# Two attention blocks on one core: PSUM tiles of the first chunks, and when the filler bank may open

## The chip, the cores and the metric

The kernel runs on one core of a Trainium2 chip. The metric is the device time of one execution in microseconds (us). The kernel before was run seven times: median 1201.62 us, lowest 1192.62, highest 1206.26 (all: 1192.62, 1201.62, 1206.26, 1194.90, 1203.48, 1195.62, 1204.34). One further execution was recorded by the hardware profiler.

Engines are named as in the profile: PE (TensorE matmul), PEld (its weight load), DVE (VectorE), ACT (ScalarE), POOL (GpSimd), SP (SyncE, which issues most transfers).

## What is computed

Two multi-head attention blocks, A and B, on different inputs of the same shape (2048 tokens, 512 features, 32 heads of 16). A attends to all tokens; B to the last 256 up to the token itself. The outputs stand side by side.

```python
qkv = (x @ wqkv).reshape(B, S, 3, H, Dh)          # S 2048, D 512, H 32, Dh 16
scores = einsum("bhqd,bhkd->bhqk", q, k) * Dh ** -0.5
# B only: scores = where(0 <= row - col < 256, scores, -1e9)
p = softmax(scores, axis=-1)
o = einsum("bhqk,bhkd->bhqd", p, v)
out = o.transpose(0, 2, 1, 3).reshape(B, S, D) @ wo
return concatenate([A, B], axis=-1)
```

## The kernel before, in words

**Jobs and slots.** A job is one head, one tile of 128 keys and up to 512 queries. Heads go in eight groups of four (`g`), queries in four passes of 512 (`p`), so a unit (instance, pass, group) of A has 64 jobs. Three jobs make a slot; there are 811 slots, and the first 21 belong to group 0 of pass 0 of A. `run` (L690) goes through them in order. In iteration s it issues: the exponentials of slot s on ACT (`exps`, L466, from PSUM tile `sps`, three banks, two buffers, into SBUF tile `pT`), the scores of slot s+2 on PE (`scores`, L448), the products with the values of earlier slots (`values`, L500, into the one-bank PSUM tile `op`), due pieces of the epilogue (`later`), then filler, and last a guard if one is due. Instructions keep this order on each engine.

**The warm matmul.** The scores of a job use 32 rows of the array; three of them stand side by side. Ahead of each slot's scores L443 issues one matmul over all 128 rows whose result is overwritten.

**Filler.** Everything else that PE must do goes into one PSUM bank, `ms` (`bank`, L113, one buffer): projections of K, Q and values, and the output projection. `pair` (L245) cuts each of these into two steps of two matmuls: the first opens the bank, the second finishes the sum and has it copied out. `plan` (L615) gives each task a due slot; `fill` (L677) issues one step of the first task that may run. `run` computes per slot the rate that the due slots ask for, adds it to `credit` (at most 2.0), and issues one step for each whole credit. A Q projection is followed two slots later by a `guard` (L304 or L400): a further matmul into `ms` whose result becomes an extra row that bounds the exponent. It is issued behind the filler of its slot, if no bank stands open.

**Padded K and Q.** The scores want each head's 16 rows at a distance of 32. Later groups get this by a trip through DRAM: the projection is copied out (L217, L297), written to scratch (`kd`, `qd`), and read back three slots later. The first two groups (`gg` 0 and 1) of A, with all keys and the first 512 queries, get it at once from padded weights `wpad` (`pad_mm`, L372). `pad_k_evac` (L382) moves the K bank to `kT` on ACT (L384, adding the constant `ones16`) and takes its largest magnitude on DVE (L386). `pad_guard` (L400) reduces and scales on DVE, then a matmul L408 and an addition L410 into the Q tile. Group 0 is done in `start`; group 1 is the task `pad` of `plan` (four K chunks, one Q), due six slots ahead of slot 21.

**The start (L550).** The tokens of A come in four chunks of 512 (L559), alternately on SP's and ACT's queue. For each chunk a three-bank `sps` tile is taken: eight transposes (L577) into its first bank, a copy by ACT to `xT`, eight into the second, a copy by DVE (L581), then four matmuls of padded K (L199) into the third, and L384 and L386. With chunk 0 the padded Q is done in `ms`. Then come the guard of group 0 and six value tiles (L594), three to an `sps` tile, each copied by ACT (L281). Then `run` issues the scores of slots 0 and 1.

**Priorities around the change.** K of pair `pr` is due 28 slots ahead of its first use, Q 22 slots ahead, value tile t of A one slot ahead, the pad task 6 slots ahead of slot 21.

Of the kernel before, what the change touches and what calls it, by code (L numbers as in the profile page):

```python
# [90 lines left out]
class _Kernel:  # L91

    def __init__(self, ctx, tc, tensors, out):
        self.tc, self.nc = tc, tc.nc
        self.t = tensors
        self.out = out
        pool = lambda name, **kw: ctx.enter_context(tc.tile_pool(name=name, **kw))
        self.consts = pool("consts", bufs=1)
        self.sb = pool("sb", bufs=1)
        self.ps = pool("ps", bufs=1, space=bass.MemoryType.PSUM)  # L100
        self.dram = pool("dram", bufs=1, space=bass.MemoryType.DRAM)
        self.xT, self.w, self.wo, self.kT, self.v, self.qT = {}, {}, {}, {}, {}, {}
        self.acol, self.negas, self.oT = {}, {}, {}
        self.op, self.od = {}, {}
        self.later = []
        self.slot = self.ended = -1
        self.pend, self.guards = [], []
        self.open = None

    def tile(self, shape, dt, tag, bufs):  # L110
        return self.sb.tile(shape, dt, name=tag, tag=tag, bufs=bufs)
# [5 lines left out]
    def constants(self):  # L117

        nc = self.nc
        pick = nc.gpsimd.affine_select  # L120
        warm = self.consts.tile([1, 1], FP32, name="warm")
        nc.vector.memset(warm[:], 0.0)
        nc.scalar.activation(out=warm[:], in_=warm[:], func=ACT.Exp)
        self.ident = self.consts.tile([P, P], BF16, name="ident")
        nc.gpsimd.memset(self.ident[:], 1.0)
        pick(self.ident[:], self.ident[:], pattern=[[1, P]], compare_op=ALU.is_equal,
             fill=0.0, base=0, channel_multiplier=-1)
        self.wpad = self.consts.tile([P, 2, NC, 2, P], BF16, name="wpad")
        nc.gpsimd.memset(self.wpad[:].bitcast(FP32), 0.0)

        sel = self.consts.tile([P, GH], FP32, name="sel")
        nc.gpsimd.memset(sel[:], 1.0)
        pick(sel[:], sel[:], pattern=[[-32, GH]], compare_op=ALU.is_equal, fill=0.0, base=-DH,
             channel_multiplier=1)
        self.ones16 = self.consts.tile([P, 1], FP32, name="ones16")
        nc.vector.reduce_sum(out=self.ones16[:], in_=sel[:], axis=AX.X)
        self.padsel = self.consts.tile([P, P], BF16, name="padsel")
        p3 = self.padsel[:].rearrange("p (j r) -> p j r", r=32)
        nc.gpsimd.memset(self.padsel[:], -1.0)
        pick(p3, p3, pattern=[[0, GH], [1, 32]], compare_op=ALU.is_equal, fill=0.0, base=-DH,  # L140
             channel_multiplier=0)
        pick(p3, p3, pattern=[[-32, GH], [0, 32]], compare_op=ALU.is_ge, fill=0.0, base=0,
             channel_multiplier=1)
        pick(p3, p3, pattern=[[32, GH], [0, 32]], compare_op=ALU.is_ge, fill=0.0, base=DH - 1,
             channel_multiplier=-1)
# [99 lines left out]
    def pair(self, first, second):  # L245

        def f():
            self.open = self.bank()
            first(self.open[:])

        def g():
            bank, self.open = self.open, None
            second(bank[:])
        return [f, g]

# [125 lines left out]

    def pad_k_evac(self, gg, c, bank):  # L382
        kT, o = self.kT[0, 0, c]
        self.nc.scalar.activation(out=kT[:, gg, o:o + 512], in_=bank, func=ACT.Identity,  # L384
                                  scale=1.0, bias=self.ones16[:])
        self.nc.vector.tensor_reduce(out=self.padmax[:, gg, c:c + 1], in_=bank, axis=AX.X,  # L386
                                     op=ALU.max, apply_absolute_value=True)

# [28 lines left out]
    def pad_steps(self):  # L417

        steps = []
        for c in range(NPASS):  # L420
            def second(bank, c=c):
                self.pad_mm(1, 1, c, bank, (2, 3))
                self.pad_k_evac(1, c, bank)
            steps += self.pair(lambda bank, c=c: self.pad_mm(1, 1, c, bank, (0, 1)), second)

        def q_second(bank):
            self.pad_mm(0, 1, 0, bank, (2, 3))
            mq = self.pad_q_evac(1, bank)
            self.guards.append((self.slot + 2, lambda: self.pad_guard(1, mq)))
        steps += self.pair(lambda bank: self.pad_mm(0, 1, 0, bank, (0, 1)), q_second)  # L430
        return steps


    def scores(self, slot):
        sps = self.ps.tile([P, SLOT, 512], FP32, name="sps", tag="sps", bufs=2)
        for b, jb in enumerate(slot["jobs"]):
            r = slice(32 * jb.j, 32 * jb.j + KR)
            qT = self.qT[jb.inst, jb.p, jb.g // 2]
            gg = jb.g % 2
            if b == 0:  # L440

                kT, k0 = self.kT[jb.inst, jb.g // 2, jb.subs[0][0] // 4]
                self.nc.tensor.matmul(sps[:, 0, 0:WARM], lhsT=kT[:, gg, k0:k0 + P],  # L443
                                      rhs=qT[:, gg, 0:WARM], start=True, stop=True)
            for kt, q0, q1, o in jb.subs:
                kT, k0 = self.kT[jb.inst, jb.g // 2, kt // 4]
                k0 += (kt % 4) * P
                self.nc.tensor.matmul(sps[:, b, o:o + q1 - q0],  # L448
                                      lhsT=kT[r, gg, k0:k0 + P],
                                      rhs=qT[r, gg, q0:q1], start=True, stop=True,  # L450
                                      tile_position=(32 * jb.j, 0))
        slot["sps"] = sps
# [97 lines left out]
    def start(self):  # L550
# [5 lines left out]
        self.load_w(0, 1, nc.scalar, (0, P))  # L556
        self.load_w(0, 0, nc.sync, (0, P))
        for c in range(NPASS):
            (nc.sync if c % 2 == 0 else nc.scalar).dma_start(xs[c // 2][:, c % 2], x[:, c])  # L559
        self.load_w(0, 2, nc.sync)  # L560
        self.load_w(0, 1, nc.scalar, (P, D))
        self.load_w(0, 0, nc.sync, (P, D))
# [3 lines left out]
                self.pad_w(n, gg)  # L566
        self.padmax = self.consts.tile([P, 2, NPASS], FP32, name="padmax")
        self.k_begin(0, 0, 0)
        for c in range(NPASS):
            big = self.ps.tile([P, SLOT, 512], FP32, name="sps", tag="sps", bufs=2)  # L570
            xT = self.tile([P, NC, 512], BF16, "xT", XRING)
            self.xT[0, c] = xT
            for h in range(2):
                tb = big[:, h, :].bitcast(BF16).rearrange("p (d n) -> p d n", d=2)
                for d in range(2):
                    for k in range(4):
                        nc.tensor.transpose(tb[:, d, k * P:(k + 1) * P],  # L577
                                            xs[c // 2][:, c % 2, k, (2 * h + d) * P:
                                                       (2 * h + d + 1) * P], self.ident[:])
                copy = nc.vector.tensor_copy if h else nc.scalar.copy  # L580
                copy(out=xT[:, 2 * h:2 * h + 2, :], in_=tb)  # L581
            self.pad_mm(1, 0, c, big[:, 2, :], range(NC))
            self.pad_k_evac(0, c, big[:, 2, :])
            if c == 0:
                b = self.bank()
                self.pad_mm(0, 0, 0, b[:], range(NC))
                mq = self.pad_q_evac(0, b[:])
        self.pad_guard(0, mq)
        self.qT[0, 0, 0] = self.padq
        nv = 2 * SLOT  # L590
        for t0 in range(0, nv, SLOT):
            vb = self.ps.tile([P, SLOT, 512], FP32, name="sps", tag="sps", bufs=2)
            for t in range(t0, t0 + SLOT):
                self.v_mm(0, t, vb[:, t - t0, :], range(NC))  # L594
                self.v_evac(0, t, vb[:, t - t0, :], nc.scalar.copy)
        self.more_constants()
        self.load_wo(0)
        return [("v", 0, t) for t in range(nv)] + [("k", 0, 0), ("q", 0, 0, 0)]
# [16 lines left out]
    def plan(self, slots, done):  # L615
# [23 lines left out]
        for t in range(NKT):  # L639
            task(("v", 0, t), vneed[0, t] - 1, self.v_steps(0, t))  # L640
        for pr in range(NPAIR):
            task(("k", 0, pr), begin[0, 0, 2 * pr] - 28, self.k_steps(0, pr, range(NPASS)))
        for i in range(2):
            for p, pr in q_order:
                old = before(q_order, (p, pr), QRING[i])
                task(("q", i, p, pr), begin[i, p, 2 * pr] - 22, self.q_steps(i, p, pr),
                     [("k", 0, pr)] if i == 0 else [("k", 1, p, pr), ("w", 1, 0)],
                     old and (i, old[0], 2 * old[1] + 1))
            for p in range(NPASS):
# [27 lines left out]
    def fill(self, s, tasks, done):  # L677

        if self.open is None:
            self.cur = next((t for t in tasks if t["nb"] <= s and t["after"] <= done), None)  # L680
            if self.cur is None:
                return False
# [7 lines left out]
    def run(self):  # L690
# [6 lines left out]
        for s, sl in enumerate(slots):  # L697
# [11 lines left out]
            for t in tasks:  # L709
                if t["nb"] <= s:  # L710
                    total += len(t["steps"])
                    rate = max(rate, total / max(1, t["due"] - s))
            credit = min(credit + min(rate, 2.0), 2.0)
            while credit >= 1.0 and self.fill(s, tasks, done):
                credit -= 1.0
            if self.guards and self.guards[0][0] <= s and self.open is None:
                self.guards.pop(0)[1]()
        finish = self.last_out(0, NPASS - 1)
        while self.pend:
            self.slot += 1  # L720
# [54 lines left out]
```

## Time and profile before

| what | us |
|---|---|
| median of seven runs | 1201.62 |
| profiled execution, its own time | 1196.32 |
| its span | 1194.6 |
| ACT busy | 1102.5 |
| PE busy (ends are modelled) | 944.6 |
| DVE busy | 293.3 |
| POOL busy | 120.0 |
| first exponential starts | 44.31 |
| exponential of slot 22 starts | 98.86 |
| mean granted PE clock, share of full | 0.941 |

How to read what follows. The slices of the page cut the span into 40 equal parts of 29.9 us, each digit the busy share in tenths. A row of the groups gives line, engine, operation, result and inputs, count, then busy us and mean ns, then the engine's idle time just ahead of these instructions and what ended most of it. A row of the waits reads: who waited, for whom, us in total, times, the longest. A row of the timeline reads: start in us, duration, engine, line, operation; in brackets how long the engine had been idle and what released it. Busy time by stretch:

| stretch, us | PE | DVE | ACT | POOL |
|---|---|---|---|---|
| 0 to 10 | 2.03 | 3.17 | 2.50 | 8.53 |
| 10 to 20 | 7.19 | 3.42 | 1.70 | 5.70 |
| 20 to 30 | 6.10 | 2.77 | 3.40 | 0 |
| 30 to 40 | 6.59 | 1.79 | 2.45 | 0 |
| 40 to 50 | 7.56 | 1.37 | 7.33 | 0 |
| 50 to 60 | 9.76 | 4.16 | 8.03 | 0 |
| 60 to 70 | 7.64 | 4.82 | 4.03 | 0 |
| 70 to 80 | 5.77 | 1.38 | 4.06 | 0 |
| 80 to 90 | 7.88 | 2.27 | 6.21 | 0 |
| 90 to 100 | 8.62 | 4.46 | 6.94 | 0 |
| 100 to 120 | 16.36 | 4.13 | 20.00 | 0 |

### The profile page before, as it was taken

To read this page: it belongs to the slowest core of one execution; us is meant where nothing else is said; L and a number is where in the kernel's file an instruction comes from. 1 tells how busy PE (TensorE), PEld (TensorE's weight loads), DVE (VectorE), ACT (ScalarE), POOL (GpSimd) and SP (SyncE) were. 2 spreads that over 40 slices of the span, in tenths; PEclk is the share of its full clock that TensorE was granted. 3 is DMA by queue.
4 is the path that set the end of the run, shared out by engine and by line. 5 is a ranking of instruction groups with operands and counts; after the bars stand their busy time and mean duration, and the time that the engine had idled before them with its cause. 6 is when DMAs were issued, how large, how long until landed. Compare 5 with 4: busy or idle time off the path is not lost.

```text
span 1194.6 us, 17547 instructions
## 1 busy us (share of the span) xinstructions
PE 944.6 (79%) x6944; PEld 272.4 (23%) x6944; DVE 293.3 (25%) x665; ACT 1102.5 (92%) x849; POOL 120.0 (10%) x316
## 2 busy tenths in 40 slices
PE   5778787887788888878788888788887888787893
PEld 3212222222222222222222222222222222222221
DVE  3223111113222213312232232133222332310101
ACT  2548999999999999999999999999999999999993
POOL 4000000001001000211011120012110111200100
PEclk9879999989999998999999999998999999979777
DMA  5011323022231202211240212123102221110101
GB/s 193 18 54 41 101 69 94 10 72 64 71 82 46 78 18 83 64 53 39 69 118 19 66 62 63 51 77 92 49 15 74 82 67 55 56 50 32 56 19 54
DMA packets 72746, 73.87 MB, mean 62 GB/s; under 512 B 22624, under 2 KB 55768, under 8 KB 72664
## 3 DMA queue, kind: packets, MB, share of 16 engines
q1 hardware_dynamic: 69624, 68.83, 19.1%
q10 hardware_dynamic: 2400, 1.84, 0.5%
q0 software_dynamic: 640, 2.10, 0.4%
q8 instruction: 54, 0.88, 0.3%
q14 instruction: 28, 0.23, 0.1%
HBM read 39.06 MB, written 31.58 MB: 59 GB/s over the span
## 4 chain that ended last, share of the span: by engine, by line
ACT 62%; PE 23%; issue 11%; DVE 2%; DMA 1%; ACTq 0%; SPq 0%; DVEq 0%
ACT pT L466 61%; PE sps L448 6%; PE sps L443 6%; PE ms L199 5%; PE op L500 4%; PE sps L199 1%; DVE osb L519 1%; PE sps L577 1%; DMA kTa<-in_A_x_dram 0%; ACT xT L581 0%; DVE pT L477 0%; PE sps L354 0%; DMA rb<-rd 0%; ACT kTa L384 0%; ACT va L281 0%
## 5 line engine op out<-in xcount | busy, mean ns | idle before, releaser
L466 ACT ACTIVATE pT<-sps 128x1536 bf16<-128x1536 f32 (+4 forms) x827 | 1087.2, 1559 | 26.0 <-PE sps L448 25.1
L443 PE MATMUL sps<-qTa,kTa 128*128 128x512 bf16 x683 | 268.3, 393 | 174.2 <-ACT pT L466 169.0
L448 PE MATMUL sps<-qTa,kTa 32*128 32x512 bf16 x2048 | 284.0, 400 | 0.0
L500 PE MATMUL op<-pT,va 128*32 128x512 bf16 x2048 | 214.2, 407 | 0.3 <-DVE osb L519 0.2
L479 POOL TENSOR_SCALAR_AFFINE_SELECT pT<-pT 128x256 bf16<-128x256 bf16 (+2 forms) x224 | 103.6, 481 | 990.2 <-issue 558.4
L448 PEld LDWEIGHTS <-kTa 32*128 32x128 bf16 x2048 | 68.1, 91 | 407.7 <-issue 407.7
L477 DVE TENSOR_TENSOR pT<-pT,mlo 128x256 bf16<-128x256 bf16 (+2 forms) x256 | 74.4, 332 | 144.0 <-ACT pT L466 142.7
L443 PEld LDWEIGHTS <-kTa 128*128 128x128 bf16 x683 | 66.6, 97 | 145.9 <-issue 124.3
L500 PEld LDWEIGHTS <-va 128*32 128x32 bf16 x2048 | 53.4, 94 | 123.3 <-issue 123.0
L443 PE MATMUL sps<-qTb,kTb 128*128 128x512 bf16 x128 | 51.7, 404 | 33.6 <-ACT pT L466 32.0
L519 DVE COPY osb<-op 128x512 f32<-128x512 f32 x64 | 44.2, 691 | 91.3 <-PE op L500 91.2
L448 PE MATMUL sps<-qTb,kTb 32*128 32x384 bf16 (+2 forms) x704 | 59.0, 292 | 0.0
L217 DVE CAST kst<-ms 128x512 bf16<-128x512 f32 x28 | 19.4, 692 | 133.9 <-PE ms L199 133.9
L339 DVE CAST ob<-ms 128x512 bf16<-128x512 f32 x28 | 19.3, 691 | 133.7 <-PE ms L199 133.7
L297 DVE CAST qs<-ms 128x512 bf16<-128x512 f32 x31 | 21.4, 690 | 105.7 <-PE ms L199 105.7
L199 PE MATMUL ms<-xT,wq 128*128 128x512 bf16 x124 | 41.5, 421 | 0.3 <-DVE gs L308 0.3
L500 PE MATMUL op<-pT,vb 128*32 128x384 bf16 (+2 forms) x704 | 36.4, 289 | 1.9 <-DVE osb L519 1.6
L448 PEld LDWEIGHTS <-kTb 32*128 32x128 bf16 x704 | 17.0, 93 | 79.1 <-issue 79.1
L199 PE MATMUL ms<-xT,wk 128*128 128x512 bf16 x112 | 34.0, 392 | 0.2 <-DVE kst L217 0.2
L281 DVE CAST vb<-ms 128x512 bf16<-128x512 f32 x16 | 11.1, 692 | 85.2 <-PE ms L199 85.2
L199 PE MATMUL ms<-wv,xT 128*128 128x512 bf16 x104 | 30.1, 387 | 0.7 <-DVE va L281 0.5
L308 DVE CAST gs<-ms 8x512 bf16<-8x512 f32 x31 | 20.9, 676 | 19.5 <-PE ms L306 19.5
(76 smaller groups left out, 290.8 us busy)
## 6 DMA issues: line engine op xcount, KB each, us to landing
od<-osb SPq DMA_DIRECT2D x64, 256.0 KB
oc<-od SPq DMA_DIRECT2D x32, 256.0 KB
rb<-rd SPq DMA_DIRECT2D x32, 256.0 KB
kTb<-kd SPq DMA_DIRECT2D x16, 256.0 KB
qTb<-qd SPq DMA_DIRECT2D x16, 256.0 KB
qd<-qs SPq DMA_DIRECT2D x31, 128.0 KB
qTa<-qd SPq DMA_DIRECT2D x15, 256.0 KB
out_dram<-ob SPq DMA_DIRECT2D x30, 128.0 KB
```

The costliest lines, as they stand in the source:

```text
L199: self.nc.tensor.matmul(bank, lhsT=lhs(c), rhs=rhs(c), start=(c == 0), stop=(c == NC - 1))
L217: copy(out=kst[:], in_=bank)
L297: copy(out=qs[:], in_=bank)
L308: self.nc.vector.tensor_copy(out=gs[:], in_=b[0:8, :])
L339: self.nc.vector.tensor_copy(out=ob[:], in_=bank)
L443: self.nc.tensor.matmul(sps[:, 0, 0:WARM], lhsT=kT[:, gg, k0:k0 + P], rhs=qT[:, gg, 0:WARM], start=True, stop=True)
L448: self.nc.tensor.matmul(sps[:, b, o:o + q1 - q0], lhsT=kT[r, gg, k0:k0 + P], rhs=qT[r, gg, q0:q1], start=True, stop=True, tile_position=(3 ...
L466: nc.scalar.activation(out=pT[:, b:e, :n], in_=sps[:, b:e, :n], func=ACT.Exp, scale=SCALE)
L477: nc.vector.tensor_mul(out=v, in0=v, in1=self.mlo[:, 0:e - b, :])
L479: nc.gpsimd.affine_select(v, v, pattern=[[0, e - b], [-1, P]], compare_op=ALU.is_ge, fill=0.0, base=-1, channel_multiplier=1)
L500: self.nc.tensor.matmul(op[32 * jb.j:32 * jb.j + 32, q0:q1], lhsT=self.v[jb.inst, kt][:, h * VP:h * VP + 32], rhs=slot["pT"][:, b, o:o + q ...
L519: nc.vector.tensor_copy(out=osb[:], in_=self.op[i, p, g][:])
```

## The change

- **Token loads.** Each chunk is loaded in two halves, one on SP's queue and one on ACT's.
- **Busy array.** 24 matmuls of 256 columns on constants (`hum`, zeros, new) into `ms` stand ahead of the first transposes on PE. Their result is not used.
- **The chunks.** All sixteen transposes of a chunk are issued together (`turn`), the two copies after them (`keep`). K chunks go to `op` and `ms` in turn (`keys`), no longer to the third bank of `sps`. The order on PE is: transposes of chunk c, then K of chunk c-1; the padded Q follows K of chunk 0.
- **Values.** Two value tiles instead of six are made in the start, each in `op`; the guard of group 0 stands between them. The other four join the filler.
- **Padded K of group 1** is moved to `kT` by DVE instead of ACT; the group 0 stays on ACT.
- **Warm matmul.** L443 is left out in slots whose preceding iteration issued two or more filler steps, and in slots 0 and 1.
- **The bank.** After a step that closes `ms`, or a guard, no new pair opens in that slot. The guard is issued ahead of the filler of its slot. The credit may rise by 2.5 a slot and to 3.0.
- **Due slots.** K is due 16 slots ahead instead of 28; Q of pass 0 of A 14 instead of 22.

```diff
@@ pair
         def g():
             bank, self.open = self.open, None
+            self.closed = self.slot
             second(bank[:])
@@ pad_k_evac
-        self.nc.scalar.activation(out=kT[:, gg, o:o + 512], in_=bank, func=ACT.Identity,
-                                  scale=1.0, bias=self.ones16[:])
+        if gg == 0:
+            self.nc.scalar.activation(out=kT[:, gg, o:o + 512], in_=bank, func=ACT.Identity,
+                                      scale=1.0, bias=self.ones16[:])
+        else:
+            self.nc.vector.tensor_scalar(out=kT[:, gg, o:o + 512], in0=bank,
+                                         scalar1=self.ones16[:], scalar2=None, op0=ALU.add)
@@ scores
-            if b == 0:
+            if b == 0 and self.filled < 2:
@@ start
-            (nc.sync if c % 2 == 0 else nc.scalar).dma_start(xs[c // 2][:, c % 2], x[:, c])
+            for h, eng in enumerate((nc.sync, nc.scalar)):
+                eng.dma_start(xs[c // 2][:, c % 2, 2 * h:2 * h + 2], x[:, c, 2 * h:2 * h + 2])
...
+        def busy(n):
+
+            b = self.bank()
+            for _ in range(n):
+                nc.tensor.matmul(b[:, 0:256], lhsT=self.padsel[:], rhs=self.hum[:],
+                                 start=True, stop=True)
+
+        def turn(c):
+            big[c] = self.ps.tile([P, SLOT, 512], FP32, name="sps", tag="sps", bufs=2)
             for h in range(2):
...
+        def keep(c):
+            xT = self.tile([P, NC, 512], BF16, "xT", XRING)
+            self.xT[0, c] = xT
+            for h in range(2):
+                tb = big[c][:, h, :].bitcast(BF16).rearrange("p (d n) -> p d n", d=2)
                 copy = nc.vector.tensor_copy if h else nc.scalar.copy
                 copy(out=xT[:, 2 * h:2 * h + 2, :], in_=tb)
...
+        def keys(c):
+            b = tile_("op", 1) if c % 2 == 0 else self.bank()
+            self.pad_mm(1, 0, c, b[:], range(NC))
+            self.pad_k_evac(0, c, b[:])
+        busy(24)
+        turn(0)
+        keep(0)
+        turn(1)
+        keys(0)
+        keep(1)
+        b = self.bank()
+        self.pad_mm(0, 0, 0, b[:], range(NC))
+        mq = self.pad_q_evac(0, b[:])
+        for c in range(2, NPASS):
+            turn(c)
+            keys(c - 1)
+            keep(c)
+        keys(NPASS - 1)
+        nv = 2
+        for t in range(nv):
+            vb = tile_("op", 1)
+            self.v_mm(0, t, vb[:], range(NC))
+            self.v_evac(0, t, vb[:], nc.scalar.copy)
+            if t == 0:
+                self.pad_guard(0, mq)
+                self.qT[0, 0, 0] = self.padq
@@ plan
-            task(("k", 0, pr), begin[0, 0, 2 * pr] - 28, self.k_steps(0, pr, range(NPASS)))
+            task(("k", 0, pr), begin[0, 0, 2 * pr] - 16, self.k_steps(0, pr, range(NPASS)))
...
-                task(("q", i, p, pr), begin[i, p, 2 * pr] - 22, self.q_steps(i, p, pr),
+                task(("q", i, p, pr), begin[i, p, 2 * pr] - (14 if i + p == 0 else 22), self.q_steps(i, p, pr),
@@ fill
         if self.open is None:
+            if self.closed == s:
+                return False
@@ run
-            credit = min(credit + min(rate, 2.0), 2.0)
+            credit = min(credit + min(rate, 2.5), 3.0)
+            self.filled = 0
+            if self.guards and self.guards[0][0] <= s and self.open is None:
+                self.guards.pop(0)[1]()
+                self.closed = s
             while credit >= 1.0 and self.fill(s, tasks, done):
                 credit -= 1.0
-            if self.guards and self.guards[0][0] <= s and self.open is None:
-                self.guards.pop(0)[1]()
+                self.filled += 1
```

More of the change, by code (lines that the diff above doesn't have):

```diff
@@ L105, in __init__ @@
         self.later = []
-        self.slot = self.ended = -1
+        self.slot = self.ended = self.closed = -1
         self.pend, self.guards = [], []
         self.open = None
+        self.filled = 2
     def tile(self, shape, dt, tag, bufs):
@@ L127, in constants @@
              fill=0.0, base=0, channel_multiplier=-1)
+        self.hum = self.consts.tile([P, 256], BF16, name="hum")
+        nc.vector.memset(self.hum[:], 0.0)
         self.wpad = self.consts.tile([P, 2, NC, 2, P], BF16, name="wpad")
@@ L428, in q_second, with guard @@
             mq = self.pad_q_evac(1, bank)
-            self.guards.append((self.slot + 2, lambda: self.pad_guard(1, mq)))
+            self.padq_done = False
+            def guard():
+                self.pad_guard(1, mq)
+                self.padq_done = True
+            self.guards.append((self.slot + 2, guard))
         steps += self.pair(lambda bank: self.pad_mm(0, 1, 0, bank, (0, 1)), q_second)
@@ L439, in scores @@
             gg = jb.g % 2
-            if b == 0:
+            assert jb.key != (0, 0, 1) or self.padq_done
+            if b == 0 and self.filled < 2:
                 kT, k0 = self.kT[jb.inst, jb.g // 2, jb.subs[0][0] // 4]
@@ L568, in start @@
         self.k_begin(0, 0, 0)
[L569 to L572, printed above, removed]
+        tile_ = lambda tag, bufs: self.ps.tile([P, 512], FP32, name=tag, tag=tag, bufs=bufs)
+        big = {}
+        def busy(n):
[5 more added lines that the diff above has]
+            big[c] = self.ps.tile([P, SLOT, 512], FP32, name="sps", tag="sps", bufs=2)
             for h in range(2):
-                tb = big[:, h, :].bitcast(BF16).rearrange("p (d n) -> p d n", d=2)
+                tb = big[c][:, h, :].bitcast(BF16).rearrange("p (d n) -> p d n", d=2)
                 for d in range(2):
@@ L579, in start @@
                                                        (2 * h + d + 1) * P], self.ident[:])
+        def keep(c):
+            xT = self.tile([P, NC, 512], BF16, "xT", XRING)
+            self.xT[0, c] = xT
+            for h in range(2):
+                tb = big[c][:, h, :].bitcast(BF16).rearrange("p (d n) -> p d n", d=2)
                 copy = nc.vector.tensor_copy if h else nc.scalar.copy
                 copy(out=xT[:, 2 * h:2 * h + 2, :], in_=tb)
[L582 to L595, printed above, removed]
+        def keys(c):
[24 more added lines that the diff above has]
+                self.qT[0, 0, 0] = self.padq
         self.more_constants()
```

## The prediction, written before the changed kernel was run

> **What bounds the kernel now.** I read the page's slices first, then ScalarE's (ACT's) waits, then the timeline of the first 100 us. The page says which engine and where:
>
> ```profile
> ACT  2548999999999999999999999999999999999993
> PEclk9879999989999998999999999998999999979777
> ...
> L466 ACT ACTIVATE pT<-sps 128x1536 bf16<-128x1536 f32 (+4 forms) x827 | 1087.2, 1559 | 26.0 <-PE sps L448 25.1
> ```
>
> From the fourth slice on ACT is busy 90% or more: the 811 slots are exponentials back to back (24 of them from 98.86 us take 32.34 us, so 1.345 us a slot). 1087.2 us of exponentials is a floor that the change does not touch. Time can be won only where ACT waits: ahead of the first exponential (44.31 us), in slices 2 to 3, in scattered gaps, and in the tail. ACT's own waits:
>
> ```profile
> ACT pT L466 <- PE sps L448: 25.1, 49, 1.9
> ACT ob L364 <- PE sps L354: 16.0, 1, 16.0
> ACT kTa L384 <- PE sps L199: 14.0, 4, 3.8
> ACT kTa L384 <- PE ms L199: 12.8, 4, 3.6
> ACT va L281 <- PE sps L199: 9.9, 6, 2.6
> ```
>
> L384 into `kTa` appears twice: in the start (sps) and inside the slots (ms). The second is 12.8 us in four waits, the largest loss inside the loop. The 16.0 us is the tail, untouched. The timeline of the start shows a ring of waits:
>
> ```profile
> 9.00 1.01 PE L577 MATMUL sps<-ident,kTa 128*128 128x128 bf16 x8 [1.10 <-ACT xT L581]
> ...
> 20.16 0.69 ACT L384 ACTIVATE kTa<-sps,ones 128x512 bf16<-128x512 f32 x1 [3.81 <-PE sps L199]
> 20.88 0.69 DVE L386 TENSOR_REDUCE padmax<-sps 128x1 f32<-128x512 f32 x1 [2.67 <-ACT kTa L384]
> ```
>
> The second eight transposes wait for ACT's copy of the first eight although they write another bank of the tile; L386 waits for L384, both reading one bank. A chunk takes 5.68 us (transposes at 14.23, 19.91, 25.59). The array runs at half rate: K matmuls follow each other at 0.427 us, against 0.216 later. Now the slots:
>
> ```profile
> 53.77 1.04 PE L199 MATMUL ms<-wv,xT 128*128 128x512 bf16 x4
> ...
> 55.59 1.02 PE L199 MATMUL ms<-wv,xT 128*128 128x512 bf16 x4 [0.24 <-DVE va L281]
> ...
> 64.74 1.04 PE L199 MATMUL ms<-xT,wpad 128*128 128x512 bf16 x4
> ...
> 65.82 0.69 ACT L384 ACTIVATE kTa<-ms,ones 128x512 bf16<-128x512 f32 x1 [3.43 <-PE ms L199]
> 66.40 1.44 ACT L466 ACTIVATE pT<-sps 128x1536 bf16<-128x1536 f32 x1
> 67.90 0.59 PE L443 MATMUL sps<-qTa,kTa 128*128 128x512 bf16 x1 [2.12 <-ACT pT L466]
> ```
>
> A slot with four filler matmuls takes 1.82 us on PE: 1.04 for the matmuls to end, 0.69 for VectorE to empty the one `ms` bank, some 0.09 between. In the padded K slots ACT stands in line for the `ms` matmuls, its next exponential behind them, and PE's next scores behind that: 5 us a slot. Slot 22 starts its exponential at 98.86, 54.55 us after slot 0; at ACT's pace it is 22 x 1.345 = 29.6. So 25.0 us are lost there: 12.8 (L384) + 7.9 (waits for scores, in that window) + four L384 at 0.58 = 23.0, the rest below what the view lists.
>
> **What the Trainium skill says.** "TensorE: Matmul & The Clock Gate", Part 1: the clock is halved until a free-running window of about 3.4 us was busy, and halved again after an idle one. The trace agrees on the two rates (0.427 and 0.216 us); but 4.4 us of PE work from 10.87 did not raise it, and gaps of 2.1 us (65.78 to 67.90) lowered it. The same page, Part 4, says that transposes do not count as busy; the start fits that. "PSUM — Partial Sum Buffer", PSUM bank collisions: two engines may not touch one bank at once, two reads included; all eight L386 wait for L384, so "one after the other" stands for the new code too. "Trainium Kernel Development and Optimization", Key Constraints: several DMA issuers share the same engines and save only issue time.
>
> **The start.** `hum` is one memset of VectorE, which otherwise waits for `sel` (1.68 us idle). Halved token loads: two more issues on each of SP and ACT, at 0.50 and 0.57 us. ACT's table load slides from 3.08 to about 4.3, the wv load on SP by 1 us; both hidden, since ACT's first copy comes near 9.8 and values near 25. Chunk 0 may land about 1.5 us earlier than 6.82: worth nothing, because PE is now held by `busy(24)`. It starts when `padsel` is ready (3.86) and takes 24 x 0.213 = 5.1 us cold (half of 0.427 for half the columns), less if the clock rises on the way: end 8.2 to 9.1, I take 8.5. So the transposes start 1.6 us later than now.
>
> From there, with rows of the trace (warm, as 27.75 to 32.7 shows): 16 transposes 1.2, ACT copy 1.01, VectorE copy 0.69, hand-overs 0.15: K chunk 0 starts 3.05 after. Each further chunk is K matmuls 1.04 + L384 0.69 + ACT copy 1.01 + VectorE copy 0.69 + hand-overs 0.2 = 3.6, transposes of the next chunk hidden beside L384. Whether VectorE's copy waits for ACT's (same tile, other bank) the trace does not show; if not, it still follows L386: about 0.35 less a chunk, 1.0 in all. Chunk 1 shares `ms` with the Q projection, whose cast comes behind chunk 1's copy: +0.8. After the last K starts: 1.04 + 0.69 + 0.69 + guard (0.6 + 0.4 + 0.69 add, value tile 1 beside it) + ACT's last value copy 0.6 and hand-overs = 5.0. Sum 3.05 + 3.6 + 0.8 + 2 x 3.65 + 5.0 = 19.75; first exponential at 8.5 + 19.75 = 28.3. All cold, the same sum (2.1 for transposes, 1.87 for K) gives 25.7, so 34.4. Half of each chunk PE idles, so I do not expect the heat of `busy` to last: I take **30.5**, ends 27.3 and 34.4. Four value tiles fewer (7.6 us, from 36.7 to 44.3) are inside this. Gain 44.3 - 30.5 = **13.8 us**.
>
> **The slots to 22.** I walked the planner's rules slot by slot. Before: value tiles 6 to 11 in slots 0 to 5, K of pair 1 in 6 to 9, padded K in 10 to 13, padded Q in 14, values 12 to 15 in 15 to 18, Q of pair 1 in 19 (the trace shows this order). After: values 2 to 11 in slots 0 to 9, padded K 10 to 13, padded Q 14, value 12 in 15, the guard alone in 16, values 13 to 15 in 17 to 19, K of pair 1 over 20 to 25, its Q in 26 and 27. As many full slots, so the four value tiles are paid by deferring K and Q.
> - Full slots: 1.82 each, `ms` turnaround. Dropping the warm matmul (0.31, L443 to L448) in 24 slots gives nothing here: PE would need about 1.63, and waits for the bank.
> - Padded K: evacuation on VectorE, 0.69 + 0.69 + 0.04, both from the bank: 1.82 + 0.73 = 2.55. Queued behind that wait on PE are the next scores; ACT waits for those. Yet 2.55 replaces about 5, and ACT loses the 0.58.
> - Guard: from value 12's matmuls to the guard's matmul 2.18 (90.17 to 92.35), to the next filler 1.17.
>
> From exponential 0 to filler 0: 2.13 - 0.31 = 1.82; then 10 x 1.82 + 4 x 2.55 + 1.82 + 3.35 + 3 x 1.82 = 39.0; the exponential of slot 22 starts 0.3 ahead of filler 20: 40.5 instead of 54.55, gain 14.0. Slots 23 to 27 now hold filler that before was done: 0.45 + 0.25 + 0.3 + 0.1 = 1.1 lost. **Net 12.9.** Against it: padded K slots keep PE 65% busy, so the clock may fall, +0.85 each (filler 1.87 for 1.04); and slot 0 may begin cold, 1 us a slot for two. I take 1.5 of the possible 5.4.
>
> **The rest.** "Open at most once" changes only two slots of 811 by the count (16 and 441). Slots with no filler go from 587 to 580, one step 204 to 210. K and Q of later pairs come up to 12 and 8 slots later; Q of pair 1 is read back in slot 32 and first needed in slot 40, 10.8 us for a transfer whose like (kd written, SP waiting for it) took 2.0 us at most. The 17.9 us of ACT gaps after 100 us are mostly falls of the clock (0.95 to 1.65 each) and stay: 0 +- 3.
>
> **Sum.** 13.8 + 12.9 - 1.5 = 25.2. The profiled execution took 1196.3, so 1171.1; the median of the seven runs is 5.3 higher and they lie in two groups 8 apart, so 1176 at the median; I take **1175**.
>
> **Rivals.** A change under 0.5% (6 us) cannot be told from none.
> 1. Forecast, 1167 to 1183: 0.55.
> 2. Cold array: 34.4 for the start, four cold padded slots, a cold entry: 9.9 + 12.9 - 5.4 = 17.4, so **1184**. For it: 70% busy was not enough before. 0.17.
> 3. Warm throughout, copies beside each other: 17.0 + 12.9 + about 3 of gaps: 33, **1168**. For it: `busy` is continuous. 0.16.
> 4. It doesn't do what it says: the tiles stay coupled, a chunk keeps its 5.68. Then only the value tiles count, 7.6 - 1.6 + 12.9 - 1.5 = 17.4, **1184**. Against: whole tiles are now written before they are read. 0.08.
> 5. Slower: the clock falls more often over the whole run, as from 1125 to 1150, where each cold slot leaves ACT idle 0.18 to 0.3 us. It decides from (25 + 6) / 0.28 = 110 more cold slots; **1208**. Against: beyond slot 27 the stream on PE is nearly the same. 0.04, a part of which only eats the gain up.
>
> Range 1165 to 1186: rivals 2 to 4 and the two groups of runs. Faster 0.95, same 0.03, slower 0.02.
>
> **What would show it.** First exponential at 27 to 34 us; L384 gone from the slots, L386 behind a VectorE add at L392 or so in `kTa`; exponentials 1.8 us apart in the first ten slots and 2.5 in the next four; slot 22 near 71 us. Wrong if the first exponential stays above 36, if padded slots take over 3.5 us, or if ACT's gaps after slot 30 exceed 22 us.

## The result, and the profile after

| | before | changed |
|---|---|---|
| median, us | 1198.89 (31 runs) | 1167.39 (12 runs, 1163.6 to 1176.0) |
| profiled execution: its time, span | 1196.32, 1194.6 | 1166.79, 1165.1 |
| first exponential starts | 44.31 | 26.05 |
| exponential of slot 22 after that of slot 0 | 54.55 | 39.96 |
| from slot 22 to slot 27 | 6.67 | 8.06 |
| from slot 27 to the end of the last exponential | 1067.1 | 1068.9 |
| from there to the end | 21.9 | 22.1 |

The ratio to the kernel before is 0.9744 (95% interval 0.972 to 0.9769): 30.7 us of 1198.9. The forecast was 1175, range 1165 to 1186. By place the 29.5 us between the two spans are 18.3 (start) + 14.6 (slots to 22) - 1.4 (slots 22 to 27) - 1.8 (rest) - 0.2 (tail). "Warm" and "cold" stand for the two rates of the array: four matmuls of 512 columns take about 1.03 us warm and 1.87 us cold.

The same lines of the page after (exponentials are L480 now):

```profile
ACT  4799999998999999999999999999999999999992
...
PEclk9999999998999999999899999998999999976777
...
L480 ACT ACTIVATE pT<-sps 128x1536 bf16<-128x1536 f32 (+4 forms) x827 | 1088.5, 1578 | 28.5 <-PE sps L462 26.9
```

ACT's second slice rises from 5 to 7, its third from 4 to 9; the floor, 1087.2, is now 1088.5. ACT's waits:

```profile
ACT pT L480 <- PE sps L462: 26.9, 61, 1.0
ACT ob L368 <- PE sps L358: 15.9, 1, 15.9
ACT L124 <- DMA kTa<-in_A_x_dram: 6.0, 1, 6.0
ACT kTa L389 <- PE ms L202: 4.3, 2, 2.5
ACT kTa L389 <- PE op L202: 2.8, 2, 1.4
ACT va L285 <- PE op L202: 2.1, 2, 1.1
```

The 12.8 us of padded K inside the slots are gone, the 14.0 of the start are 7.1, the value copies 2.1 instead of 9.9. The first row has not become smaller. The start, in the timeline (transposes L600, their copies L610, K matmuls L202):

```profile
8.20 1.95 PE L600 MATMUL sps<-ident,kTa 128*128 128x128 bf16 x32
9.29 1.01 ACT L610 COPY xT<-sps 128x1024 bf16<-128x1024 bf16 x1 [1.79 <-PE sps L600]
10.33 0.69 DVE L610 COPY xT<-sps 128x1024 bf16<-128x1024 bf16 x1 [3.62 <-ACT xT L610]
10.35 1.32 PE L202 MATMUL op<-xT,wpad 128*128 128x512 bf16 x4 [0.21 <-ACT xT L610]
...
14.68 1.04 PE L202 MATMUL ms<-xT,wpad 128*128 128x512 bf16 x4 [1.25 <-DVE qTa L402]
...
17.39 1.32 PE L202 MATMUL op<-xT,wpad 128*128 128x512 bf16 x4 [0.79 <-ACT xT L610]
...
20.39 1.74 PE L202 MATMUL ms<-xT,wpad 128*128 128x512 bf16 x4 [1.68 <-ACT xT L610]
...
26.05 8.30 ACT L480 ACTIVATE pT<-sps 128x1536 bf16<-128x1536 f32 x6
```

K chunks start 4.33, 2.71 and 3.00 us apart, against 5.68 for a chunk before. VectorE's copy does wait for ACT's, one way that the trace before had left open. But K starts beside VectorE's copy: its first two matmuls need only ACT's half. And a padded slot:

```profile
45.95 1.02 PE L202 MATMUL ms<-xT,wpad 128*128 128x512 bf16 x4
...
47.01 0.75 DVE L392 TENSOR_SCALAR kTa<-ms,ones 128x512 bf16<-128x512 f32 x1 [1.11 <-PE ms L202]
...
47.68 0.68 DVE L394 TENSOR_REDUCE padmax<-ms 128x1 f32<-128x512 f32 x1
48.41 1.02 PE L202 MATMUL ms<-xT,wpad 128*128 128x512 bf16 x4 [0.79 <-DVE padmax L394]
...
49.87 1.45 ACT L480 ACTIVATE pT<-sps 128x1536 bf16<-128x1536 f32 x1 [1.01 <-PE sps L462]
```

From filler to filler it is 2.46 us (2.55 forecast), and PE waits for the second read of the bank.

### The profile page after: what moved, and what is told of

The parts are those of the page before. It is cut to its first block, busy times and chain, and to the rows that moved or that the text cites. A ratio compares the mean times of both kernels' runs of the same rounds, so it can differ in the third digit from the quotient of the medians.

```text
span 1165.1 us, 17551 instructions
## 1 busy us (share of the span) xinstructions
PE 936.9 (80%) x6944; PEld 270.8 (23%) x6944; DVE 299.9 (26%) x674; ACT 1098.7 (94%) x841; POOL 119.2 (10%) x316
## 3 DMA queue, kind: packets, MB, share of 16 engines
q10 hardware_dynamic: 2432, 1.84, 0.5%
## 4 chain that ended last, share of the span: by engine, by line
ACT 63%; PE 22%; issue 10%; DVE 4%; DMA 1%; POOL 0%; ACTq 0%; SPq 0%; DVEq 0%; POOLq 0%
ACT pT L480 62%; PE sps L462 6%; PE sps L457 6%; PE ms L202 5%; PE op L514 4%; DVE va L285 1%; DVE osb L533 1%; PE ms L591 0%; DMA den<-od 0%; DMA rb<-rd 0%; ACT xT L610 0%; PE sps L358 0%; DVE padmax L394 0%; DVE pT L491 0%; DVE kTa L392 0%
## 5 line engine op out<-in xcount | busy, mean ns | idle before, releaser
L480 ACT ACTIVATE pT<-sps 128x1536 bf16<-128x1536 f32 (+4 forms) x827 | 1088.5, 1578 | 28.5 <-PE sps L462 26.9
L457 PE MATMUL sps<-qTa,kTa 128*128 128x512 bf16 x659 | 259.5, 394 | 158.3 <-ACT pT L480 152.6
L457 PEld LDWEIGHTS <-kTa 128*128 128x128 bf16 x659 | 64.1, 97 | 142.4 <-issue 122.1
L202 PE MATMUL ms<-xT,wq 128*128 128x512 bf16 x124 | 40.1, 408 | 0.4 <-DVE gs L312 0.3
L202 PE MATMUL ms<-wv,xT 128*128 128x512 bf16 x120 | 34.2, 385 | 2.7 <-DVE va L285 1.3
L202 PE MATMUL ms<-xT,wk 128*128 128x512 bf16 x112 | 35.7, 405 | 0.7 <-DVE kst L220 0.5
```

What stands on the lines that cost most here:

```text
L202: self.nc.tensor.matmul(bank, lhsT=lhs(c), rhs=rhs(c), start=(c == 0), stop=(c == NC - 1))
L480: nc.scalar.activation(out=pT[:, b:e, :n], in_=sps[:, b:e, :n], func=ACT.Exp, scale=SCALE)
```

## The experiments

"After slot 0" means from the start of slot 0's exponential to that of slot 22. Ratios are to the kernel before, run alongside; where two intervals overlap, the totals are not told apart.

**Without the busy array.**

```diff
-        busy(24)
```

> The changed kernel without the 24 matmuls ahead of the first transposes. Changed kernel: first transposes 8.20, first exponential 26.05, slot 22 at 66.01 us. Theory (the array's heat shortens the start): transposes begin near 5.5 when chunk 0 lands, but at half rate, K matmuls 0.427 us apart; PE then needs about 4 us a chunk and the first exponential comes at 28 to 30, total some 3 us longer. Rival (the copies on ACT and DVE pace the start, the heat is spent before it counts): the start moves up by the 2.7 us that PE is free earlier, first exponential near 23.5, total 2 to 3 us shorter.

Measured: 1166.31 us, ratio 0.9736 (0.9707 to 0.9765); first exponential 25.53, slot 22 41.24 after slot 0.

```profile
5.51 3.89 PE L600 MATMUL sps<-ident,kTa 128*128 128x128 bf16 x32 [5.51 <-DMA kTa<-in_A_x_dram]
...
9.19 1.83 PE L202 MATMUL op<-xT,wpad 128*128 128x512 bf16 x4
10.86 1.03 PE L202 MATMUL ms<-xT,wpad 128*128 128x512 bf16 x4
```

Neither theory held as put. The 32 transposes take twice as long (3.89 against 1.95) and K of chunk 0 is cold (1.83 for four), but the four matmuls behind it already run at full rate (1.03): in the new order PE works from 5.51 us without a pause, and the trace's record of the clock rises to full at 10.8. The 24 matmuls cost the 2.7 us that they hold PE and give about that back: the first exponential is 0.5 us earlier without them, which is less than the spread of the five profiled executions whose start is the changed one (25.7 to 26.9). Their worth here is nothing that can be measured.

**Padded K of group 1 on ACT again.**

```diff
-        if gg == 0:
+        if gg < 2:
             self.nc.scalar.activation(out=kT[:, gg, o:o + 512], in_=bank, func=ACT.Identity,
```

> The changed kernel with the padded K of group 1 moved out by ACT again (both groups on ACT). Theory (ACT standing in line for the filler's matmuls is what made these slots 5 us): the four padded slots go from 2.46 back to about 5.2 us, slot 22 some 51 us after slot 0 instead of 39.96, total 10 to 11 us longer, near 1178. Rival (one bank emptied by two reads limits them wherever the first read is): within 2 us of the changed kernel.

Measured: 1179.0 us, ratio 0.9844 (0.9816 to 0.9872); slot 22 50.8 after slot 0.

```profile
47.48 0.69 ACT L389 ACTIVATE kTa<-ms,ones 128x512 bf16<-128x512 f32 x1 [3.57 <-PE ms L202]
48.06 1.44 ACT L480 ACTIVATE pT<-sps 128x1536 bf16<-128x1536 f32 x1
52.58 0.69 ACT L389 ACTIVATE kTa<-ms,ones 128x512 bf16<-128x512 f32 x1 [3.08 <-PE ms L202]
```

The 5.1 us slots are back, by one line of code: 10.8 us in this stretch. The theory holds in size.

**The same line alone, in the kernel before.** The edit is the change's own `pad_k_evac`, nothing else.

> The kernel before with one part of the change: padded K of group 1 moved out by VectorE. Theory: first exponential stays at 44.3; the four padded slots go from 5.2 to about 2.5 us, slot 22 some 43.5 us after slot 0 instead of 54.55, total 11 us shorter than before. Rival (the bank rule, the credit and the dropped warm matmul bring a good part of the slots' gain): slot 22 above 48 us.

Measured: 1188.39 us, ratio 0.991 (0.9878 to 0.9942); slot 22 42.66 after slot 0.

```profile
82.29 1.45 ACT L470 ACTIVATE pT<-sps 128x1536 bf16<-128x1536 f32 x1 [1.92 <-PE sps L452]
```

So of the slots' 14.6 us, 11.9 come from this line alone. Of the other 2.7, 1.6 are the wait in this row, where the guard shares the bank with a value tile in one slot; in the changed kernel ACT waits 0.29 us there. The experiment after next brings it back.

**The warm matmul kept.**

```diff
-            if b == 0 and self.filled < 2:
+            if b == 0:
```

> The changed kernel with the warm matmul in every slot again. Theory (full slots wait for the bank, 1.81 us, and PE with the warm matmul needs 1.84): slot 22 at 39.96 + 0.5 to 1 us after slot 0, total within 1.5 us. Rival (PE's own work sets the full slots): 0.31 us in each of 22 slots, total 6 to 7 us longer.

Measured: 1172.07 us, ratio 0.9762 (0.9724 to 0.9801); slot 22 40.81 after slot 0, 0.85 later, mostly at the entry (slots 3 to 5); the full slots are 1.84 apart instead of 1.81. As the theory said, a matmul that runs while PE would wait for the bank costs almost nothing. The total is not told apart from the changed kernel's.

**The bank rule undone.**

```diff
-            if self.closed == s:
-                return False
...
-            credit = min(credit + min(rate, 2.5), 3.0)
+            credit = min(credit + min(rate, 2.0), 2.0)
...
-            if self.guards and self.guards[0][0] <= s and self.open is None:
-                self.guards.pop(0)[1]()
-                self.closed = s
             while credit >= 1.0 and self.fill(s, tasks, done):
                 credit -= 1.0
                 self.filled += 1
+            if self.guards and self.guards[0][0] <= s and self.open is None:
+                self.guards.pop(0)[1]()
```

> The changed kernel with the second part of the change undone: a pair may open in the slot in which another closed, guards come behind the filler of their slot, credit rises by at most 2.0 to at most 2.0. Theory (the count of filler steps shows only two slots of 811 where the bank was opened twice): slot 22 within 1 us, total within 2 us. Rival (the rule is what keeps PE from waiting for the bank): stalls of 0.7 us or more in many of the first 28 slots, total 5 us or more longer.

Measured: 1170.61 us, ratio 0.977 (0.9745 to 0.9796); slot 22 41.54 after slot 0. Here, and then in the changed kernel:

```profile
59.49 1.45 ACT L480 ACTIVATE pT<-sps 128x1536 bf16<-128x1536 f32 x1 [0.35 <-PE sps L462]
62.82 1.45 ACT L480 ACTIVATE pT<-sps 128x1536 bf16<-128x1536 f32 x1 [1.88 <-PE sps L462]
```

```profile
60.81 3.04 ACT L480 ACTIVATE pT<-sps 128x1536 bf16<-128x1536 f32 x2 [0.29 <-PE sps L462]
```

One stall, where a value tile and the guard use the bank in one slot: ACT waits 1.88 us there, 0.29 in the changed kernel. So the bank rule, the guard's place and the credit together are worth 1.6 us at slot 22, a little above the 1 us expected, and 0.9 by slot 27; the rival's many stalls do not appear. The profiled execution's further 5 us (1074.1 from slot 27 on) came with a mean clock of 0.933 against 0.943, and no place in the code is tied to them; the two intervals overlap.

**Six value tiles in the start.**

```diff
-        nv = 2
+        nv = 6
```

> The changed kernel with six value tiles in the start instead of two. Theory (moving four value tiles into slots that wait anyway trades about 1.7 us each in the start, matmuls 0.87 + hand-over 0.2 + ACT copy 0.6, for 1.81 - 1.345 = 0.46 each in the slots): first exponential at 32.5 to 33, slot 22 some 38 us after slot 0, total 4 to 5 us longer than the changed kernel. Rival (work on PE is only shifted): start longer and slots shorter by the same, total within 1.5 us.

Measured: 1171.44 us, ratio 0.9765 (0.972 to 0.981); first exponential 33.98, slot 22 40.12 after slot 0. The four tiles take 6.8 us (copies at 26.71 to 33.50, 1.70 apart), as expected. The slots did not get shorter, though 38 us had been expected: ACT waits 1.46 us in an early one, where four filler matmuls took 1.89 instead of 1.02, the array being cold (the clock's record has half rate from 36.5 to 43.3). At slot 27 the loss is 7.2 us; that the total's 4 to 5 agrees with the expectation is partly luck, because the rest of that execution was 2 us shorter.

**The chunk loop of before, two value tiles.** The start's functions are replaced by the old loop (L569 to L589), values 0 and 1 in one `sps` tile behind the guard, no matmuls ahead; all else as changed.

> The changed kernel with the chunk loop of the kernel before (copies between the transposes, K in the third bank of the same tile, no matmuls ahead) and two value tiles. Theory (the overlap of chunks is worth what the value tiles don't explain, 18.3 - 7.6 = 10.7 us): first exponential at 36 to 38, slots as in the changed kernel, total 10 to 11 us longer than the changed kernel. Rival (fewer value tiles and earlier tokens are most of the start's gain): first exponential below 31.

Measured: 1183.37 us, ratio 0.9856 (0.982 to 0.9893); first exponential 35.27, slot 22 43.59 after slot 0.

```profile
5.84 1.03 PE L592 MATMUL sps<-ident,kTa 128*128 128x128 bf16 x8 [5.84 <-DMA kTa<-in_A_x_dram]
...
8.86 1.01 PE L592 MATMUL sps<-ident,kTa 128*128 128x128 bf16 x8 [1.98 <-ACT xT L596]
...
34.62 1.35 PE L462 MATMUL sps<-qTa,kTa 32*128 32x512 bf16 x6
```

The tokens come 1.0 us earlier than in the kernel before (5.84 against 6.87); nothing but the halved loads differs ahead of them, though these were not tried alone. With the value tiles (7.6) this makes 44.31 into about 35.3; the new loop, with all that goes with it, is worth the other 9.2 us. The total missed the expectation by 5 us. For 3.6 of them I had left out what the old loop leaves behind, a cold array: scores of slot 0 at half rate (1.35 us for six matmuls, 0.60 in the changed kernel), and longer first slots. Some 2 us came after slot 27 and are tied to no place.

**K of the start in the third bank again.**

```diff
-            b = tile_("op", 1) if c % 2 == 0 else self.bank()
-            self.pad_mm(1, 0, c, b[:], range(NC))
-            self.pad_k_evac(0, c, b[:])
+            self.pad_mm(1, 0, c, big[c][:, 2, :], range(NC))
+            self.pad_k_evac(0, c, big[c][:, 2, :])
```

> The changed kernel with the K chunks of the start in the third bank of their chunk's own tile again, the order of issue as changed. Theory (the new order, all sixteen transposes first and the next chunk's ahead of K, brings the overlap; where K lies matters little): K of chunk 1 no longer waits for the bank of the padded Q (1.25 us saved), transposes of chunk 2 wait some 1 us for the largest-magnitude read of chunk 0; first exponential within 1 us of 26.05. Rival (separate tiles bring the overlap): first exponential at 29 or later.

Measured: 1169.85 us, ratio 0.9784 (0.9762 to 0.9807); first exponential 27.88, between the theory's 27.05 and the rival's 29. But here the transposes began at 9.01 instead of 8.20, as the 24 matmuls took longer to become warm; from the transposes it is 18.87 us, against 17.85 in the changed kernel (17.85 to 18.06 in the five executions with its start).

```profile
11.25 0.69 DVE L610 COPY xT<-sps 128x1024 bf16<-128x1024 bf16 x1 [4.93 <-ACT xT L610]
11.99 1.02 PE L202 MATMUL sps<-xT,wpad 128*128 128x512 bf16 x4 [0.93 <-DVE xT L610]
```

So of the new loop's 9.2 us, separate tiles bring 0.8 to 1.0; the other 8 or so come with the order of issue and the rest of the new start. How much of them is the overlap and how much the warmer array (K of chunks 0 and 2 took 1.86 us in the old loop) was not separated. The rows show how a shared tile costs: in one tile, K waits for VectorE's copy of the transposes although it writes another bank; in its own tile it starts after ACT's.

**The largest magnitude from SBUF.**

```diff
         self.nc.vector.tensor_reduce(out=self.padmax[:, gg, c:c + 1],
-                                     in_=bank, axis=AX.X,
+                                     in_=kT[:, gg, o:o + 512], axis=AX.X,
```

> The changed kernel with the largest magnitude of padded K taken from kT in SBUF instead of from the bank, so that the bank is free after its first read (the constant row is not used by the guard). Theory (turnaround of the one bank sets these slots): the four padded K slots go from 2.46 to 1.81 us, slot 22 at 37.3 us after slot 0 instead of 39.96, total 2.6 us shorter. Rival (VectorE's two operations or PE set them): no change of these slots.

Measured: 1165.41 us, ratio 0.9715 (0.9684 to 0.9745); slot 22 37.56 after slot 0, 2.4 less. The total is not told apart from the changed kernel's.

```profile
48.77 0.69 DVE L394 TENSOR_REDUCE padmax<-kTa 128x1 f32<-128x512 bf16 x1
48.78 1.02 PE L202 MATMUL ms<-xT,wpad 128*128 128x512 bf16 x4 [0.19 <-DVE kTa L392]
...
50.65 1.02 PE L202 MATMUL ms<-xT,wpad 128*128 128x512 bf16 x4 [0.19 <-DVE kTa L392]
```

Same two operations on VectorE, but PE no longer waits for the second: 1.87 from filler to filler. The turnaround of the one bank sets these slots, as the theory said.

**Both of the last two.**

> The changed kernel with K of the start in the third bank and the largest magnitude of padded K taken from kT in SBUF. Theory: padded slots at 1.85 us, slot 22 at 37.4 us after slot 0, first exponential 25 to 26.5 us, total 2.5 to 4 us shorter than the changed kernel. Rival: the two do not add, within 1 us of the version with the read from SBUF alone (1165.4).

Measured: 1166.23 us, ratio 0.975 (0.9732 to 0.9768); first exponential 27.32, slot 22 37.91 after slot 0. They do not add: K in the third bank is a loss, not a gain (from the first transposes to the first exponential again 18.88 us).

**Two warm matmuls.** The first row of ACT's waits had stayed, so I asked what its gaps are.

```diff
-                self.nc.tensor.matmul(sps[:, 0, 0:WARM], lhsT=kT[:, gg, k0:k0 + P],
-                                      rhs=qT[:, gg, 0:WARM], start=True, stop=True)
+                for _ in range(2 - self.filled):
+                    self.nc.tensor.matmul(sps[:, 0, 0:WARM], lhsT=kT[:, gg, k0:k0 + P],
+                                          rhs=qT[:, gg, 0:WARM], start=True, stop=True)
```

> The changed kernel with two warm matmuls ahead of the scores where the preceding iteration issued no filler, one where it issued one step, none where it issued two. Theory (ACT's gaps after slot 27, 18.5 us in the changed kernel, are falls of the array's clock, which come where PE is busy too little): with 0.22 us more in a slot that has 0.37 us to spare the gaps fall below 10 us and the total by about 8 us. Rival (the clock falls for another reason than too little work): gaps as before, total the same or longer.

Measured: 1150.95 us, ratio 0.9619 (0.96 to 0.9637). ACT's listed gaps after slot 27 are 3.8 us instead of 18.5, and the stretch from slot 27 to the last exponential 1051.3 instead of 1068.9. In the changed kernel the clock's record has 18 stretches at half rate, 136 us in all, and 16.9 of the 18.5 us of gaps lie inside one or within 0.5 us behind it. With two warm matmuls it has two, one ahead of the first exponential and one behind the last, and none in the slots. The page's clock, and the stretch from 1030 to 1080 us (PE, PEld, DVE, ACT, POOL busy, then the clock), first of this kernel:

```profile
PEclk9999999999999999999999999999999999999996
```

```profile
1030.00:1080.00 50.00, 43.60 (x344) 14.06 (x344) 8.38 (x23) 50.00 (x39) 6.45 (x14) 1.00 0.13 41
```

and of the changed kernel:

```profile
1030.00:1080.00 50.00, 45.14 (x283) 10.52 (x282) 6.63 (x16) 48.02 (x35) 5.82 (x13) 0.68 0.06 20
```

With more matmuls PE is busy for less time there, because each runs at full rate, and ACT never waits (the two stretches do not hold just the same slots, this kernel being some 17 us ahead). The gain is twice what I expected, because the gaps went almost wholly, where I had expected them to fall below 10 us. They make 14.7 of the 17.6 us. For the other 2.9 there is an estimate: exponentials in a row start 1.33 us apart but last 1.45 or more, so a wait costs some 0.1 us beyond its gap, and there are 33 fewer waits.

**Both gains.** Two warm matmuls and the largest magnitude from SBUF.

> The version with two warm matmuls and the largest magnitude of padded K taken from kT in SBUF. Theory (the two gains lie in different stretches, slots 10 to 13 and the slots after 27, so they add): slot 22 at 37.4 us after slot 0, total 2 to 3 us below the version with two warm matmuls alone (1150.95), so near 1148.5. Rival (they do not add): within 1 us of 1151.

Measured: 1147.77 us (1147.48 to 1148.81), ratio 0.9584 (0.9561 to 0.9608); slot 22 37.56 after slot 0. In their places the gains add (from slot 27 to the last exponential again 1051.3); the intervals of this total and of the one with two warm matmuls alone overlap. This version is faster than both kernels.

## Why the prediction was right, point by point

- **Sign, size and the two places: right.** 25.2 us were forecast, 29.5 came in the profiled pair. 1167.39 lies in the range, 7.6 below the forecast: 4.3 of this is the gain, and 3.3 the step from the profiled execution to the median, forecast as 3.9 and measured as 0.6. That rival 3 ("warm throughout, copies beside each other", 1168) came nearer is chance: the copies did not lie beside each other, and the array was cold from 21.0 to 24.4 us and in 17 stretches later.
- **The slots: right, and shown.** Slot 22 at 40.5 was forecast, 39.96 measured; padded slots 2.55 against 2.46; from value tile 12 over the guard to the next filler 3.35 against 3.33; the loss in slots 22 to 27 1.1 against 1.4. That the dropped warm matmul gives next to nothing (0.85 us) is shown by keeping it, that the bank rule gives little by undoing it, and that one moved copy gives most of the 14.6 by moving it alone (11.9) and back (10.8).
- **The start: mis-sized by 4.4 us** (30.5 forecast, 26.05 measured, below even the lower end of 27.3). Half is the 2.2 us allowed for a cold array, on which the next point speaks. The other half is the chain. Its failed term is "K matmuls 1.04 + L384 0.69 + ACT copy 1.01 + VectorE copy 0.69" a chunk, 3.6: VectorE's copy does come behind ACT's, but lies beside K's first matmuls, so the last two chunks took 2.71 and 3.00. I had taken the copies as the question and not asked which half of `xT` each K matmul reads. The same slip made K of chunk 0 start 3.05 after the first transposes; it was 2.15. That the step to chunk 1 came out (4.4 forecast, 4.33 measured) is luck: the wait for the padded Q's bank was longer than the 0.8 allowed. The chain from the last K to the first exponential took 5.66 instead of 5.0, the array being cold again there (1.74 us for the last K instead of 1.04). The all-cold end is 8.5 + 25.7 = 34.2, not 34.4, which changes nothing.
- **"I do not expect the heat of `busy` to last": wrong in effect.** The array stayed warm until 21.0 us, which made 2.2 us of my 30.5 needless. But not by `busy` alone: without it the array was warm from 10.8 us, and the first exponential came at 25.53. The reading that transposes do not count as busy is not borne out either: a warm array did them in half the time (1.95 against 3.89 us for 32), and without `busy` the clock rose after 3.7 us of transposes and only 1.6 us of matmuls.
- **The clock allowance of 1.5 us in the slots was not needed**: no padded slot was cold in this execution. It was a real risk: without `busy`, the padded Q's four matmuls took 1.87 us (at 55.28), and slot 22 came 1.3 later after slot 0.
- **The rest, 0 +- 3: right** (1.8 us longer). That these gaps "are mostly falls of the clock" was argued; the two warm matmuls show it.
- **Rival 4** fell: the chunks do overlap, 2.71 and 3.00 us apart, though K in a tile of its own brings only 0.8 to 1.0 us of it.
- **Open**: why just these moments lose the clock in an execution. In the changed kernel 65 of the 116 us at half rate inside the slots come after 1000 us, and from 1000 to 1110 us only 6 matmuls of the projections run, against 30 to 50 in every 100 us before. That fits too little work on PE; but from 200 to 800 us the clock falls and from 800 to 1000 it does not, at about the same number. The later due slots of K and Q were not tried alone; with K at its old 28 slots and only two value tiles made in the start, the planner puts value tile 12 behind its first use.

## What to carry to other kernels

When an engine that sets the pace also empties a PSUM bank, its own work stands in line behind the matmuls that fill that bank; give the copy to an engine with slack, and let its first read free the bank (here 11 to 12 us for the one, 2.4 for the other). Cost a chain of copies by what each matmul reads, not by the tile. And where PE has spare time in each slot, look at the granted clock before calling the gaps noise: work without a result, put where PE idles, was worth 16 us here, more than half of what the change was.

## What the runs showed that I had not expected

- The array's clock fell in a steady stream without long pauses: in the 7 us ahead of each of the 16 falls inside the slots of the changed kernel, PE's longest pause was 0.3 to 0.7 us. In a slot without filler, scores, values and one warm matmul make about 0.97 of 1.345 us, and the mean clock of that kernel was 0.943. With one 0.22 us matmul more a slot (about 1.18 of 1.345) it was 0.991 in all four executions, and the profiled one had no fall in the slots.
- In all 14 traces every stretch at half rate lasts 3.41 us or a whole multiple of it, but for the last one of each, which runs into the end.
- Much of the spread between runs goes with this clock: of the twelve runs of the changed kernel the four slowest (1171.4 to 1176.0 us) have 0.927 to 0.936, the other eight (1163.6 to 1167.8) 0.937 to 0.947, without a strict order among these. With two warm matmuls the runs lie within 1148.94 to 1151.64.
- The clock's record begins with the first rise (26.9 us in the kernel before, 7.3 in the changed one), and the page counts all ahead of it as full rate. So this row of the kernel before ends in a clock of 1.00 (before the DMA share and GB/s), while its K matmuls stand 0.427 us apart: at the start the rate is read from the matmuls.

```profile
10.00:20.00 10.00, 7.19 (x30) 3.51 (x29) 3.42 (x5) 1.70 (x2) 5.70 (x33) 1.00 0.88 318
```

- The first rise itself moves: in the five executions with the changed start, the 24 matmuls began at 3.9 us and the clock rose at 6.7 to 8.7, so that the transposes began at 7.9 to 8.9.
- At entry into the slots a cold array costs about 2 us (six value tiles, against the 38 expected) to 3.6 us (old loop).
